# The scaling of the attention probabilities moves to GpSimd in the first 32 of 72 attention steps

## The chip, the cores and the metric

The kernel runs on one core of a Trainium2 chip. Time is device microseconds (us) of one execution; the kernel before took 945.74 us (median of three runs, 944.77 to 946.35). One execution was recorded by the hardware profiler; its rows are used below. PE is TensorE, DVE VectorE, ACT ScalarE, POOL GpSimd; SP issues the DMAs.

## The reference, cut to what matters

```python
# q, k, v: (4, 8, 576, 64) float32
scores = q @ k^T / sqrt(64) - 2**-(h+1) * |i - j|      # head h, masked to 0 <= i - j < 128
attn   = exp(scores - max(scores))
attn   = attn / (sum(attn) + 1e-9)                       # the normalisation in question
x      = (attn @ v) as (2304 tokens, 512)
x      = relu(x @ w1_in)**2 @ w1_out                     # 512 -> 2048 -> 512
h      = x @ w2_in
out    = (h * cos(h)) @ w2_out
```

All in float32.

## The kernel before, in words

**Attention.** The 2304 tokens are 18 tiles of 128; the 8 heads are 4 pairs. One attention *step* (`a`, or `s`) is one tile and one pair of heads, so there are 72 steps, four to a tile. Step a does, in `scores` (L309): matmuls on PE into a bank of PSUM (tile `s_a`), for each of the two heads one custom DVE reduction (L367: adds the bias table, finds the row's extreme), and one ACT exponential (L377) that writes the probabilities `p_a` to SBUF and the row sums to a small tile `st_a`. `normalise` (L386) then makes 1/(sum + 1e-9) on DVE with two instructions on 128x2 (L389, L390), and multiplies each head's 128x256 probabilities by it (L393): two `tensor_scalar` instructions per step, on DVE, over 128 columns in the first tile's four steps, 192 in steps 20 to 23 (tile 5) and 256 elsewhere. `transposes` (L395) turns the four 128x128 blocks on PE (`t_a`) and ACT copies them back into `p_a` (L404). `values` (L407) multiplies by v (`o`); after four steps ACT and DVE split the tile's result into a rounded part `xh` and a rest `xl` (L433, L434), the operands of the first layer.

**MLPs.** A unit i is 128 of the 2048 hidden columns by 512 tokens: 12 matmuls (`h_i`, L463 to L465: three products of rounded parts and rests for each of four slices), the activation, and 12 more (`y`, L524 to L526). The weights arrive as 64-bit floats and are converted piecewise: a POOL memset of a buffer `cv_w` (L168), an ACT cast (L175), a DVE shift-and-or (L179), an ACT cast to the rounded part `wh` (L192) and a DVE subtraction for the rest `wl` (L196). There are two `cv_w` buffers, so a memset waits for the `wl` of two pieces before.

**Order.** The code first runs the *start stage*: steps 0 to 15 back to back, scores up to two steps ahead (`LOOK`). From step 16 on, one step is woven into each unit; steps 16 to 31 lie beside units 0 to 15. The code gives a priority; a scheduler then builds a fixed order of instructions for each engine, with waits on semaphores, from estimated costs, so an edit can move instructions of all engines. Each engine then works through its own list in that order; a waiting instruction holds up all behind it.

**Buffers that tie steps together.** `st` has four buffers: the reductions of step a+4 can't begin until step a's multiplications have read `st_a`. The keys of tile 3 and the keys and queries of tiles 4 and later come by DMA through two buffers `raw_a` (`kq_job`, L251): ACT casts them into `KS` and `qh` (L264, L277, L278), DVE subtracts (`KS`, L265 and L282; `ql`, L283), and only then can the load two further on begin. Below, raw_a0 to raw_a3 are the four loads for tile 3 and raw_a4 to raw_a7 those for steps 16 to 19.

Of the kernel before, what the change touches and what calls it, by code (L numbers as in the profile page):

```python
# [15 lines left out]
ALU = mybir.AluOpType  # L16
# [53 lines left out]
def attention_mlp_mlp(ctx: ExitStack, tc: tile.TileContext, kq, k0, q0, v, w1, w2, bias, ident, out):  # L70
# [7 lines left out]
    te, act, dve, pool, sp = nc.tensor, nc.scalar, nc.vector, nc.gpsimd, nc.sync  # L78
# [216 lines left out]
    def kind(j):  # L295
        return {0: "first", 4: "straddle", 5: "after"}.get(j % 9, "plain")
# [89 lines left out]
    def normalise(a):  # L386
        j, hp = divmod(a, 4)
        pt, st = Pt[a], St.pop(a)
        dve.tensor_scalar(st[:, 4:6], st[:, 2:4], 1e-9, None, ALU.add)  # L389
        dve.reciprocal(st[:, 6:8], st[:, 4:6])  # L390
        c0, c1 = {"first": (0, 128), "after": (64, 256)}.get(kind(j), (0, 256))
        for e in range(2):
            dve.tensor_scalar(pt[:, e, c0:c1], pt[:, e, c0:c1], st[:, 6 + e : 7 + e], None, ALU.mult)  # L393

    def transposes(s):  # L395
        j, hp = divmod(s, 4)
# [184 lines left out]
    with ExitStack():  # L581
# [43 lines left out]
        while s < start_steps:  # L625
            scores_to(min(s + LOOK, start_steps))
            normalise(s)
            transposes(s)
            tick("aw" if s < START_W else "a")
            values(s)  # L630
            s += 1
# [8 lines left out]
        for i in range(len(ORDER)):  # L640
# [9 lines left out]
            if todo > 0:  # L650
                scores_to(s + 1)
                normalise(s)
# [29 lines left out]
            for _ in range(todo - 1):  # L682
                scores_to(s + 1)
                normalise(s)
                transposes(s)
                tick()
                values(s)
                vdone[0] = s + 1
                s += 1
# [57 lines left out]
```

## Time and profile before

| | |
|---|---|
| median of three runs | 945.74 us |
| the profiled execution | 946.06 us, of which the profiler's span is 944.3 us |
| PE busy | 921.9 us, 98% of the span |
| DVE, ACT, POOL busy | 599.4, 522.9, 43.3 us |
| start stage | to about 54 us; there PE is idle for about 14 us |

A share of busy time is an average over the stages; the end of a matmul is modelled, so a busy PE isn't PE at its peak. "Granted clock" is a share of full speed.

### The profile page before, as it was taken

To read this page: it belongs to the slowest core of one execution; us is meant where nothing else is said; L and a number is where in the kernel's file an instruction comes from. 1 tells how busy PE (TensorE), PEld (TensorE's weight loads), DVE (VectorE), ACT (ScalarE), POOL (GpSimd) and SP (SyncE) were. 2 spreads that over 40 slices of the span, in tenths; PEclk is the share of its full clock that TensorE was granted. 3 is DMA by queue.
4 is the path that set the end of the run, shared out by engine and by line. 5 is a ranking of instruction groups with operands and counts; after the bars stand their busy time and mean duration, and the time that the engine had idled before them with its cause. 6 is when DMAs were issued, how large, how long until landed. Compare 5 with 4: busy or idle time off the path is not lost.

```text
span 944.3 us, 13513 instructions
## 1 busy us (share of the span) xinstructions
PE 921.9 (98%) x4992; PEld 768.4 (81%) x4992; DVE 599.4 (63%) x1403; ACT 522.9 (55%) x1134; POOL 43.3 (5%) x100
## 2 busy tenths in 40 slices
PE   7789999999999999999999999999999999999998
PEld 6567777778787888878888888888888888888898
DVE  4988896666657655555655686566556555655564
ACT  4988885554556645455545574454445444444443
POOL 2011110000000000000101100000000000000000
PEclk9999999999999999999999999999999999999999
DMA  7545663320112111123342440011001000100010
GB/s 215 190 168 190 213 219 98 108 68 34 56 57 101 45 38 53 46 85 116 121 147 89 158 155 1 1 45 45 1 1 40 5 1 1 45 1 1 1 45 23
DMA packets 33954, 71.44 MB, mean 76 GB/s; under 512 B 3424, under 2 KB 10976, under 8 KB 33888
## 3 DMA queue, kind: packets, MB, share of 16 engines
q1 hardware_dynamic: 33888, 70.58, 22.6%
q8 instruction: 39, 0.64, 0.3%
q14 instruction: 27, 0.22, 0.1%
HBM read 61.13 MB, written 9.44 MB: 75 GB/s over the span
## 4 chain that ended last, share of the span: by engine, by line
PE 88%; ACT 4%; DVE 4%; DMA 3%; issue 1%; SPq 0%; POOL 0%; ACTq 0%; DVEq 0%
PE h L464 13%; PE h L463 13%; PE h L465 13%; PE y L524 13%; PE y L525 13%; PE y L526 13%; PE s L335 3%; PE o L419 3%; PE t L402 2%; DMA raw_a<-kq_in 2%; ACT p L377 1%; PE s L324 1%; DVE s L367 1%; ACT cv_w L175 1%; DVE cv_w L179 1%
## 5 line engine op out<-in xcount | busy, mean ns | idle before, releaser
L463 PE MATMUL h<-xh,wh 128*128 128x512 f32 (+1 forms) x640 | 237.3, 371 | 0.6 <-ACT xh L433 0.4
L464 PE MATMUL h<-xl,wh 128*128 128x512 f32 (+1 forms) x640 | 236.8, 370 | 0.3 <-DVE xl L434 0.3
L465 PE MATMUL h<-xh,wl 128*128 128x512 f32 (+1 forms) x640 | 236.3, 369 | 0.0
L463 PEld LDWEIGHTS h<-xh,wh 128*128 128x128 f32 x640 | 121.2, 189 | 20.2 <-ACT a L469 0.7
L465 PEld LDWEIGHTS h<-xh,wl 128*128 128x128 f32 x640 | 121.1, 189 | 20.3
L464 PEld LDWEIGHTS h<-xl,wh 128*128 128x128 f32 x640 | 121.1, 189 | 19.0 <-DVE xl L434 0.7
L524 PE MATMUL y<-rh,wh 128*128 128x512 f32 (+1 forms) x320 | 122.5, 383 | 0.8 <-DVE ysb L539 0.8
L525 PE MATMUL y<-rl,wh 128*128 128x512 f32 (+1 forms) x320 | 118.5, 370 | 0.0
L526 PE MATMUL y<-rh,wl 128*128 128x512 f32 (+1 forms) x320 | 118.4, 370 | 0.0
L524 PE MATMUL y<-gh,wh 128*128 128x512 f32 (+1 forms) x320 | 117.8, 368 | 0.0
L525 PE MATMUL y<-gl,wh 128*128 128x512 f32 (+1 forms) x320 | 117.7, 368 | 0.0
L526 PE MATMUL y<-gh,wl 128*128 128x512 f32 (+1 forms) x320 | 117.7, 368 | 0.0
L492 ACT ACTIVATE r<-r 128x512 f32<-128x512 f32 x72 | 45.4, 631 | 120.0 <-DVE r L491 120.0
L377 ACT ACTIVATE p<-s,st 128x256 f32<-128x256 f32 (+4 forms) x160 | 70.6, 443 | 49.3 <-DVE st L367 47.3
L503 DVE TENSOR_TENSOR gl<-r,gh 128x512 fp32r<-128x512 f32 x72 | 49.8, 691 | 75.1 <-ACT gh L502 75.0
L367 DVE CUSTOM_DVE_ANT_0 s<-s,bias_sb 128x256 f32<-128x256 f32 (+4 forms) x160 | 62.1, 392 | 55.5 <-PE s L335 27.1
L489 DVE SCALAR_TENSOR_TENSOR r<-kk,h 128x512 f32<-128x512 int32 x72 | 49.4, 687 | 68.0 <-ACT kk L488 68.0
L488 ACT ACTIVATE kk<-h 128x512 int32<-128x512 f32 x72 | 43.0, 597 | 75.6 <-PE h L465 75.5
L480 DVE TENSOR_TENSOR a<-a 128x512 f32<-128x512 f32 x62 | 42.8, 691 | 49.0 <-ACT rh L479 46.8
L469 ACT ACTIVATE a<-h 128x512 f32<-128x512 f32 x72 | 42.9, 596 | 51.4 <-PE h L465 50.4
L526 PEld LDWEIGHTS y<-rh,wl 128*128 128x128 f32 x320 | 60.3, 188 | 10.5
L524 PEld LDWEIGHTS y<-rh,wh 128*128 128x128 f32 x320 | 60.4, 189 | 9.9 <-DVE ysb L539 1.3
(60 smaller groups left out, 1389.3 us busy)
## 6 DMA issues: line engine op xcount, KB each, us to landing
raw_w<-w_in SPq DMA_DIRECT2D x64, 511.8 KB, 4.6
raw_a<-kq_in SPq DMA_DIRECT2D x56, 256.0 KB, 2.6
v<-v_in SPq DMA_DIRECT2D x18, 256.0 KB, 3.4
y<-ysb SPq DMA_DIRECT2D x18, 256.0 KB, 2.0
raw_a<-y SPq DMA_DIRECT2D x18, 256.0 KB, 2.7
out<-ysb SPq DMA_DIRECT2D x16, 256.0 KB, 2.5
k<-k_in SPq DMA_DIRECT2D x4, 256.0 KB, 5.5
q<-q_in SPq DMA_DIRECT2D x8, 128.0 KB, 5.6
```

The costliest lines, as they stand in the source:

```text
L367: dve.tensor_tensor_reduce(out=sbank[p0:p1, e, c0:c1], in0=sbank[p0:p1, e, c0:c1], in1=bias_sb[p0:p1, h, b0 + c0 : b0 + c1], scale=-0.125, ...
L377: act.activation(pt[p0:p1, e, c0:c1], sbank[p0:p1, e, c0:c1], AF.Exp, bias=st[p0:p1, e : e + 1], scale=-1.0, accum_out=st[p0:p1, 2 + e : 3 ...
L463: te.matmul(o, wh[:, cs], xh, start=(c == 0 and kt == 0), stop=False, skip_group_check=True)
L464: te.matmul(o, wh[:, cs], xl, start=False, stop=False, skip_group_check=True)
L465: te.matmul(o, wl[:, cs], xh, start=False, stop=(kt == KT - 1), skip_group_check=True)
L488: act.activation(kk, hb, AF.Copy, scale=INV2PI)
L489: dve.scalar_tensor_tensor(r, kk, -C1, hb, ALU.mult, ALU.add)
L492: act.activation(r, r, AF.Abs)
L503: dve.tensor_tensor(rl, r, rh.bitcast(F32), ALU.subtract)
L524: te.matmul(o, wh, gh, start=(first and m % per == 0), stop=False, skip_group_check=True)
L525: te.matmul(o, wh, gl, start=False, stop=False, skip_group_check=True)
L526: te.matmul(o, wl, gh, start=False, stop=last, skip_group_check=True)
```

## The change

In `normalise`, the two multiplications of a step go to POOL for steps 0 to 31: 64 instructions. The reciprocal stays on DVE. The remaining 40 steps are as before.

```diff
         c0, c1 = {"first": (0, 128), "after": (64, 256)}.get(kind(j), (0, 256))
+
+        engine = pool if a < 32 else dve
         for e in range(2):
-            dve.tensor_scalar(pt[:, e, c0:c1], pt[:, e, c0:c1], st[:, 6 + e : 7 + e], None, ALU.mult)
+            engine.tensor_scalar(pt[:, e, c0:c1], pt[:, e, c0:c1], st[:, 6 + e : 7 + e], None, ALU.mult)
```

Two lines are added, so every line below L391 has a number two higher in the changed kernel (L393 is L395, L402 is L404). POOL's list of instructions about the end of its first memsets, before:

```order
L363 MEMSET p_18_768 64x2x128
L168 MEMSET cv_w_0_1_0_667 128x512
L168 MEMSET cv_w_0_1_1_700 128x512
L168 MEMSET cv_w_0_2_0_745 128x512
L168 MEMSET cv_w_0_2_1_789 128x512
```

and at the same place now (`p_0` holds the probabilities of steps 0 and 1, `p_2` those of 2 and 3, and so on):

```order
L363 MEMSET p_18_768 64x2x128
L395 ISA
L395 TENSOR_SCALAR p_0_166<-p_0_166,st_0_167 128x128 x2
L395 TENSOR_SCALAR p_0_166<-p_0_166,st_1_175 128x128 x2
L395 TENSOR_SCALAR p_2_183<-p_2_183,st_2_184 128x128 x2
L395 TENSOR_SCALAR p_2_183<-p_2_183,st_3_211 128x128 x2
L395 TENSOR_SCALAR p_4_234<-p_4_234,st_4_235 128x256 x2
L395 TENSOR_SCALAR p_4_234<-p_4_234,st_5_259 128x256 x2
L395 TENSOR_SCALAR p_6_290<-p_6_290,st_6_291 128x256 x2
L395 TENSOR_SCALAR p_6_290<-p_6_290,st_7_318 128x256 x2
L168 MEMSET cv_w_0_1_0_667 128x512
L168 MEMSET cv_w_0_1_1_700 128x512
```

The multiplications stand in POOL's list among the memsets. The row that reads only ISA is new too: in the built program it is a reload of a library of POOL's code, put once ahead of the first multiplication; the list before has no such row.

PE's list at the start of the attention (`s_4` to `s_6` are scores of steps 4 to 6, `t_0` the transposes of step 0), before:

```order
L324 MATMUL s_4_229<-k0_0_129,q0_1_132 128x128 x2
L402 MATMUL t_0_193<-id_sb_126,p_0_166 128x128
L324 MATMUL s_4_229<-k0_0_129,q0_1_132 128x128
L402 MATMUL t_0_193<-id_sb_126,p_0_166 128x128
L324 MATMUL s_4_229<-k0_0_129,q0_1_132 128x128
L419 MATMUL o_0_205<-p_0_166,v_0_147 64x128 x2
L324 MATMUL s_5_254<-k0_0_129,q0_1_132 128x128 x4
```

and now:

```order
L324 MATMUL s_4_229<-k0_0_129,q0_1_132 128x128 x4
L324 MATMUL s_5_254<-k0_0_129,q0_1_132 128x128 x4
L324 MATMUL s_6_285<-k0_0_129,q0_1_132 128x128 x4
L404 MATMUL t_0_193<-id_sb_126,p_0_166 128x128 x2
L404 MATMUL t_1_220<-id_sb_126,p_0_166 128x128 x2
```

The scores of steps 4, 5 and 6 have moved ahead of the first transposes.

PE's list where the start stage ends and the first unit begins (`h_0`), before:

```order
L335 MATMUL s_17_674<-KS_127,ql_4_1_514 128x256 x2
L463 MATMUL h_0_652<-xh_0_100,wh_0_0_272 128x512
L464 MATMUL h_0_652<-xl_0_101,wh_0_0_272 128x512
L465 MATMUL h_0_652<-xh_0_100,wl_0_0_273 128x512
L463 MATMUL h_0_652<-xh_0_100,wh_0_0_272 128x512
```

and now:

```order
L335 MATMUL s_17_674<-KS_127,ql_4_1_514 128x256 x2
L404 MATMUL t_16_732<-id_sb_126,p_16_596 128x128 x4
L465 MATMUL h_0_652<-xh_0_100,wh_0_0_272 128x512
L335 MATMUL s_18_763<-KS_127,qh_4_2_550 128x256 x2
L335 MATMUL s_18_763<-KS_127,ql_4_2_551 128x256 x2
L466 MATMUL h_0_652<-xl_0_101,wh_0_0_272 128x512
```

The transposes of step 16 and the scores of step 18 now stand ahead of the second matmul of unit 0; before they stood behind unit 0 and behind the first `y` matmuls. From unit 3 on, PE's list is the same in both kernels. On DVE the conversions of unit 1's weights have moved from the middle of the start stage to its end, just ahead of the split of tile 3.

## Rows read from the trace of the kernel before

**Rows 1.** The page, busy time and share of the span

```profile
PE 921.9 (98%) x4992; PEld 768.4 (81%) x4992; DVE 599.4 (63%) x1403; ACT 522.9 (55%) x1134; POOL 43.3 (5%) x100
```

**Rows 2.** Windows: stretch, length, busy per engine (x instructions), granted clock, DMA share, GB/s

```profile
0.00:60.00 60.00, 45.64 (x305) 35.99 (x306) 44.18 (x179) 42.60 (x127) 10.30 (x27) 0.94 0.65 200
60.00:160.00 100.00, 96.05 (x531) 77.78 (x532) 81.17 (x216) 83.62 (x196) 14.54 (x31) 1.00 0.56 184
160.00:944.00 784.00, 780.20 (x4158) 654.65 (x4156) 474.01 (x1008) 396.66 (x812) 18.48 (x42) 1.00 0.16 52
20.00:30.00 10.00, 9.88 (x88) 8.25 (x86) 9.50 (x40) 9.80 (x27) 1.06 (x2) 1.00 0.48 162
30.00:40.00 10.00, 7.65 (x70) 5.63 (x70) 9.48 (x40) 9.26 (x30) 0.00 (x0) 1.00 0.65 208
40.00:50.00 10.00, 5.86 (x46) 4.13 (x44) 8.45 (x28) 7.76 (x23) 1.13 (x2) 0.83 0.32 107
```

Busy times stand in the order PE, PE's weight loads, DVE, ACT, POOL.

**Rows 3.** Timeline of PE: start, length, instruction, idle before and its releaser

```profile
43.99 0.66 PE L419 MATMUL o<-p,v 128*64 128x128 f32 x8 [2.40 <-DVE xl L434]
...
53.94 0.49 PE L463 MATMUL h<-xh,wh 128*128 128x512 f32 x1 [0.36 <-ACT xh L433]
...
54.78 0.73 PE L464 MATMUL h<-xl,wh 128*128 128x512 f32 x1 [0.34 <-DVE xl L434]
```

**Rows 4.** DVE's multiplications to 160 us, by shape: busy, mean ns

```profile
L393 DVE TENSOR_SCALAR p<-p,st 128x256 f32<-128x256 f32 x46 | 15.1, 364 | 0.5
...
L393 DVE TENSOR_SCALAR p<-p,st 128x128 f32<-128x128 f32 x8 | 1.9, 283 | 0.0
```

**Rows 5.** POOL's memsets by shape: busy, mean ns, idle before

```profile
L168 POOL MEMSET cv_w<- 128x512 f32 x64 | 33.8, 529 | 310.1 <-DVE wl L196 296.8 <-DVE st L389 7.1 <-DVE st L390 5.4
L363 POOL MEMSET p<- 64x256 f32 x8 | 2.5, 311 | 0.0
```

**Rows 6.** Timeline, first 10 us: the load of ACT's table, POOL's last memset, DVE's first multiplications

```profile
0.73 1.28 ACT L377 ACT_TABLE_LOAD   x1 [0.73 <-PEq L736]
...
7.18 0.31 POOL L363 MEMSET p<- 64x256 f32 x1
...
9.18 0.48 DVE L393 TENSOR_SCALAR p<-p,st 128x128 f32<-128x128 f32 x2
```

**Rows 7.** The page, DMA issues: count, KB each, median us to landing

```profile
q<-q_in SPq DMA_DIRECT2D x8, 128.0 KB, 5.6
```

**Rows 8.** Timeline: the keys' loads and conversions (SP, ACT, DVE) from 30 us

```profile
30.55 0.42 DVE L265 TENSOR_TENSOR KS<-raw_a,KS 64x256 fp32r<-64x256 f32 x1
...
42.04 6.27 SPq L287 DMA_DIRECT2D raw_a<-kq_in  x3
...
45.10 0.40 ACT L277 CAST KS<-raw_a 128x256 fp32r<-128x256 f32 x1
...
46.56 0.42 DVE L367 CUSTOM_DVE_ANT_0 s<-s,bias_sb 64x256 f32<-64x256 f32 x1 [0.94 <-PE s L335]
...
47.08 0.42 DVE L282 TENSOR_TENSOR KS<-raw_a,KS 64x256 fp32r<-64x256 f32 x1
```

**Rows 9.** Timeline of PE: step 16's transposes, step 18's scores

```profile
58.98 0.60 PE L402 MATMUL t<-id_sb,p 128*128 128x128 f32 x4
...
65.41 0.40 PE L335 MATMUL s<-KS,qh 128*128 128x256 f32 x2
```

**Rows 10.** Timeline about 82 us: DVE's reciprocal of a step, PE's transposes of it

```profile
81.90 0.17 DVE L390 RECIPROCAL st<-st 128x2 f32<-128x2 f32 x1
...
84.60 0.60 PE L402 MATMUL t<-id_sb,p 128*128 128x128 f32 x4
```

**Rows 11.** Timeline: the same DVE instruction alone, then beside a POOL memset

```profile
87.00 0.17 DVE L389 TENSOR_SCALAR st<-st 128x2 f32<-128x2 f32 x1 [0.58 <-ACT p L377]
...
94.83 0.53 POOL L168 MEMSET cv_w<- 128x512 f32 x1 [2.77 <-DVE wl L196]
94.88 0.50 DVE L389 TENSOR_SCALAR st<-st 128x2 f32<-128x2 f32 x1
```

## The prediction, on record before the changed kernel ran

> **What bounds the kernel now.** I read the page first, then windows, then the timeline about the start stage. PE is busy for 98% of the span [rows 1], so only PE's idle time can be saved. The windows say where that lies: PE idles 14.4 us of the first 60, 3.9 us of the next 100 and 3.8 us of the last 784 [rows 2]. The first few of the 14.4 are the wait for the first data. Most of the rest falls at 30 to 60 us, where DVE and ACT are busy for 8 to 9.5 of each 10 us [rows 2] and PE waits for DVE in turn: 2.40 us for the split of a tile, then again before the first unit [rows 3]. The granted clock, 0.83 of full speed in 40 to 50 us against 1.00 before, also shows a PE that stands still too often [rows 2]. So the stage to read is the start stage, steps 0 to 15, which ends with the second matmul of unit 0 at 54.78 us [rows 3]. It is the second that counts: from there PE hardly stops.
>
> From 60 us on DVE is busy 81%, but off the path. I expect nothing from the 16 later steps' relief there (16 x 2 x 0.36 = 12 us of DVE): PE's whole idle time is 3.9 us in that stretch, and the order from unit 3 on is unchanged.
>
> **What is removed.** In the start stage, 8 multiplications of 283 ns and 24 of 364 ns [rows 4]: 2.3 + 8.7 = 11 us of DVE's 44.2 busy in 60 [rows 2]. This is a profiled length with the next instruction overlapping it: two over 128 columns together took 0.48 us [rows 6], so the relief of the queue is nearer 9 us. It lies on the path only where PE waits for DVE.
>
> **What is added.** Three things, none of which the trace shows.
>
> 1. *A multiplication on POOL.* The nearest rows are POOL's memsets, which only write: 311 ns for 256 columns, 529 ns for 512 [rows 5]. The lower bound is 0.31 us (reading costs nothing); the upper is twice 529, 1.06 us. I take 0.53 us, as if it touched 512 columns: 256 read, 256 written. A step then costs POOL 1.06 us. The start stage has one step in 2.85 us (54.78 - 9.18 for 16 [rows 3, 6]), so POOL has the room, and the price is latency: a step's transposes begin some 0.5 us later after the reciprocal than with two DVE instructions.
>
> 2. *The reload of POOL's library.* It stands in POOL's list behind the memset that ends at 7.49 us, and all multiplications stand behind it. The first was needed at 9.18 us [rows 6], so the first 1.7 us are free. The only loading of code or tables that the trace shows is ACT's table, 1.28 us [rows 6]; that is the lower bound. If it needs a transfer from memory, the slowest median from issue to landing is the queries', 5.6 us [rows 7]; twice that, 11.2 us, is the upper bound. I take 5.6: code has to come from memory, and this is the stretch in which those loads were measured. The first multiplication then starts at 7.5 + 5.6 = 13.1 us, 3.9 us late.
>
>    The Trainium skill, in GPSIMD Engine Reference, section 2.1, says that the first call to a freshly loaded kernel costs an extra load of about 6 us, measured as 5.95, with no instruction shown for it. No row here shows it; by that figure the sum below would be 0.35 us worse.
>
> 3. *Waits in other queues.* On POOL the memsets of weight buffers now stand between multiplications. Each waits for a DVE `wl` that stands ahead of the reciprocal for which the next multiplication waits, so a step costs at most one memset more (0.53 us). On SP no load moves past a multiplication; but a `raw_a` load waits for DVE's subtractions, and these have moved.
>
> **What the late start costs.** Until 13.1 us DVE, ACT and PE can do the reductions and exponentials of steps 0 to 3 and the scores of steps 4 to 6, which now stand ahead of the first transposes. Then all of them stop, for want of a free `st`. So PE loses less than 3.9 us: about two and a half steps of scores, some 3 us, are taken ahead. Walking the new orders with the lengths of before, step 8's scores end at about the same time as before (some 21 us), with the transposes of step 4 still owed. From there DVE has less to do.
>
> **Where the gain goes.** The second half of the stage hangs on a chain that the change doesn't shorten: the key loads through two buffers. A load for step 18 is issued at 42.04 us, when step 16's subtraction is done, and its cast begins at 45.10 [rows 8]: 3.1 us a link, four links from raw_a0 to raw_a8. The first link starts with the subtraction at 30.55 us [rows 8]. In DVE's new list that subtraction stands behind the split of tile 1 and the first reduction of step 12, and I put it at 31.7 us, 1.1 us later. On the way the lighter DVE gives this back. Before, DVE stood before step 16's reduction until PE had the scores at 46.56, and only then subtracted step 18's keys at 47.08, 1.6 us after their cast was ready [rows 8]. PE had those scores late because the transposes of step 13 waited for DVE. Now I put step 16's reduction at 43.5, and step 18's subtraction right behind its cast, at 46.4: 0.7 us earlier than before. From there to the second matmul of unit 0 it was 54.78 - 47.08 = 7.7 us; DVE's list between them loses 4 multiplications of before (some 1.2 us), but PE must now first do step 16's transposes, which wait for two POOL multiplications and a memset, and step 18's scores, which together take the 1.0 us back. So the second matmul comes at about 53.9, 0.9 us earlier. What stands ahead of it needn't be done later: four transposes, 0.60 us long with the next matmul overlapping (0.45), and scores of about the same length [rows 9], 0.9 us.
>
> Step 16 to 31: between the end of a step's reciprocal and its transposes the tightest place that I found has 84.60 - 82.07 = 2.5 us [rows 10]; two POOL multiplications, a memset and 0.2 us for the signals are 1.8 us. Nothing is lost.
>
> **Sum.** -0.9 - 0.9 = -1.8 us against the profiled execution's 946.06 us (the span of 944.3 and 1.8 around it): 944.3. That execution was 0.3 us above the median of the runs, so against 945.74 the forecast is 943.9 us: a small gain, just at the edge of what can be told from no change here, 0.2% or 1.9 us.
>
> **The rivals.**
>
> *A. The reload is free.* If the code is resident, or comes in ACT's 1.28 us, the first multiplication starts on time and the late start of 3.9 us is gone. PE had filled 1 us of it with work taken ahead, so 2.9 us more come off: 941.0 us. For it: PE's idle time in 30 to 60 us has room for it. Against: the load would have to be shorter than any transfer here.
>
> *B. The reload is long (slower).* Every microsecond beyond 5.6 passes on whole, since DVE, ACT and PE stop behind `st` and the key chain starts later by the same. At 7.4 us the gain is gone; from 9.3 us on the kernel is slower by over 0.2%. At 11.2 us: 943.9 + 5.6 = 949.5. For it: nothing else on POOL can run behind it, and the loads at this time share the DMA with 200 GB/s of other traffic [rows 2]. Against: only that other loads land in half the time.
>
> *C. POOL and DVE hold each other up (slower).* A DVE instruction of 0.17 us took 0.50 when a POOL memset began 0.05 us ahead of it [rows 11]: it waited the memset out. The multiplications will do the same to DVE's remaining small ones, and be held in turn. If each of the last ten of the start stage loses 0.27 us (half of 0.53) on the path, it is 2.7 us, and 946.6. At 1.06 us a multiplication, 5.3 us: 949.2. For it: the row. Against: DVE has 9 us less to do, so waits on it fall into slack except in the tail.
>
> The skill's SBUF — State Buffer, section "Who interferes with whom", makes this an exclusive lock, and adds that a DVE instruction with two SBUF inputs also contends with a POOL instruction that reads SBUF. With the first [rows 11] agree; the second no row of before can show, as POOL only wrote. By it the subtractions (`wl`, `KS`, `ql`) would be held up as well, which is rival C at its upper price.
>
> That the change doesn't do what it says is excluded: the 64 instructions stand in POOL's list.
>
> **How the numbers follow.** The forecast gets 0.42, with a range of its own of 941.5 to 945.5 (0.31 to 1.06 us a multiplication, the reload 4 to 7 us); it lies astride the edge, so 0.20 of it is faster and 0.22 no change. A 0.20, all faster. B 0.22: 0.18 slower, 0.04 no change. C 0.16: 0.10 slower, 0.06 no change. Together 0.40 faster, 0.32 no change, 0.28 slower. The range, 939.5 to 950.5, takes in A with 1.5 us to spare below, B and C to their upper bounds.
>
> **What would show it.** *Reload:* the first POOL multiplication at about 13.1 us; at 9 us it is A, beyond 17 us B. *Length:* POOL multiplications 0.3 to 1.06 us. *Chain:* the first key subtraction near 31.7 us, step 18's near 46.4. *End of the stage:* unit 0's second matmul near 53.9 us, and afterwards the same distance to the end as before, less 0.9 us. *Lock:* 128x2 instructions on DVE of 0.5 us instead of 0.17 in the start stage. The forecast is wrong if the second matmul comes after 55.7 us, or if PE idles more than 5 us between 60 and 160 us.

## The result, and the profile after

The changed kernel takes 956.41 us (median of 4 runs, 952.66 to 957.83) beside 946.05 us for the kernel before on the same chip: a ratio of 1.0099, 95% interval 1.0076 to 1.0121, or about 9.4 us (7.2 to 11.4) slower. The forecast was 943.9 us with a range up to 950.5. The profiled execution took 957.2 us, 11.1 more than that of before, with a span of 955.4 us. Lines behind L391 of the changed kernel stand two further down: the multiplication is L395, the transposes are L404, the first unit's matmuls L465 to L467.

The page's line of busy times, the answer to [rows 1]. DVE has lost 12 us and POOL has gained 59:

```profile
PE 927.8 (97%) x4992; PEld 769.9 (81%) x4992; DVE 587.0 (61%) x1339; ACT 523.7 (55%) x1134; POOL 102.4 (11%) x164
```

The windows, with the columns of [rows 2]:

```profile
0.00:60.00 60.00, 42.08 (x284) 32.29 (x284) 31.87 (x128) 35.72 (x111) 35.81 (x56) 0.86 0.54 161
60.00:160.00 100.00, 94.29 (x501) 74.06 (x500) 75.57 (x187) 85.86 (x197) 41.87 (x61) 0.97 0.61 197
...
20.00:30.00 10.00, 7.42 (x58) 5.33 (x57) 6.11 (x23) 7.55 (x23) 6.33 (x7) 1.00 0.31 100
30.00:40.00 10.00, 8.21 (x73) 6.03 (x72) 5.54 (x23) 6.85 (x21) 6.04 (x9) 1.00 0.29 86
```

From 20 to 30 us PE has fallen from 9.88 to 7.42, and DVE, which was full at 9.50, to 6.11; ACT has fallen too. POOL itself is busy for only 6.3 of the 10 us. Nobody is full any more: the stage waits on its own chain. How late it ends is read on PE's timeline (start, length, idle before, releaser; compare [rows 3]):

```profile
62.18 0.78 PE L465 MATMUL h<-xh,wh 128*128 128x512 f32 x1
...
64.29 0.63 PE L466 MATMUL h<-xl,wh 128*128 128x512 f32 x1
```

The second matmul of unit 0 comes 9.5 us later than before (64.29 against 54.78), which is most of the 11.1. (Between kernels with another order on PE its time is no measure by itself: other work stands ahead of it.) What POOL's multiplication costs stands in the groups by shape (busy us, mean ns), the answer to [rows 4, 5]:

```profile
L395 POOL TENSOR_SCALAR p<-p,st 128x256 f32<-128x256 f32 x48 | 48.3, 1019 | 37.6 <-DVE st L390 19.6 <-DVE st L389 4.5 <-ACT p L406 4.3
...
L395 POOL TENSOR_SCALAR p<-p,st 128x128 f32<-128x128 f32 x8 | 4.7, 603 | 4.8 <-DVE st L390 4.7 <-DVE st L389 0.2
```

The mean also holds slower ones; over the start stage it is 0.974 us. The fastest, four back to back, last 3.62 us, 0.905 each, in the timeline of all engines about 23 us:

```profile
21.30 3.62 POOL L395 TENSOR_SCALAR p<-p,st 128x256 f32<-128x256 f32 x4 [4.30 <-ACT p L406]
...
22.27 0.44 PE L404 MATMUL t<-id_sb,p 128*128 128x128 f32 x2 [0.16 <-POOL p L395]
23.15 0.43 DVE L367 CUSTOM_DVE_ANT_0 s<-s,bias_sb 128x256 f32<-128x256 f32 x1 [1.76 <-POOL p L395]
...
23.17 0.44 PE L404 MATMUL t<-id_sb,p 128*128 128x128 f32 x2 [0.46 <-POOL p L395]
...
29.65 0.43 DVE L367 CUSTOM_DVE_ANT_0 s<-s,bias_sb 128x256 f32<-128x256 f32 x1 [0.84 <-POOL p L395]
```

Two things are to be seen. PE's transposes follow POOL's multiplications one by one, 0.90 us apart, and PE stands still 0.46 us between them. And DVE's *reduction* of a later step, which has nothing to do with that product, stood 1.76 us and then 0.84 us until POOL was done: it writes the row maximum into a tile `st`, there are four of them, and POOL reads the reciprocal out of the oldest until a step's second multiplication ends. DVE's waits up to 70 us (waited for: us in total, times, longest) have three such waits:

```profile
DVE s L367 <- PE s L324: 12.1, 5, 6.3
DVE st L389 <- ACT p L377: 4.1, 5, 2.2
DVE s L367 <- POOL p L395: 3.7, 3, 1.8
```

The wait for PE's scores grew more. Before, it was

```profile
DVE s L367 <- PE s L324: 6.5, 2, 6.1
```

Without the longest in each, which is the wait for the first data, that is 0.4 us before and 5.8 us now. The chain that ended last before 66 us shows which of the two counts (start, length, what):

```profile
21.30 3.63 POOL p L395 x4
24.97 0.44 PE t L404 x2
25.41 0.34 PE s L324 x4
25.76 0.68 issue
26.44 0.43 DVE s L367
27.01 0.11 DVE st L390
27.29 2.34 POOL p L395 x2
29.67 0.44 PE t L404 x2
```

It goes from POOL's product to PE's transposes of step 5, from there to the scores of step 9, which stand behind those transposes in PE's list, to the reduction of these scores, to the reciprocal of step 6, which stands behind that reduction in DVE's list, and back to POOL. Such rounds make up the chain from 21 to 47 us, and POOL's multiplications are 12.4 of its 66 us. No piece of it leads from POOL to a reduction: the three waits for `st` are there, but not on it. The longest wait of a reduction after the first data shows the path once more, between the transposes of step 9 and the scores of step 12:

```profile
37.32 0.44 PE L404 MATMUL t<-id_sb,p 128*128 128x128 f32 x2 [0.46 <-POOL p L395]
...
37.59 0.83 PE L324 MATMUL s<-k,q 128*128 128x128 f32 x6
...
38.13 0.43 DVE L367 CUSTOM_DVE_ANT_0 s<-s,bias_sb 128x256 f32<-128x256 f32 x1 [2.53 <-PE s L324]
```

An estimate says the same. If all starts are worked out again from the lengths in this trace and the waits in the built program, leaving out only the reductions' waits for POOL, the second matmul stays at 64.29 us (in the start-only, half-columns and two-halves kernels below it stays where it was, too). With POOL's multiplications 0.58 as long, near the forecast's 1.06 us a step, it comes at 58.5 us.

Behind that the key chain is late as well, the answer to [rows 8] (DVE's subtractions, first and step 18's):

```profile
38.65 0.76 DVE L265 TENSOR_TENSOR KS<-raw_a,KS 64x256 fp32r<-64x256 f32 x2
...
54.62 0.42 DVE L282 TENSOR_TENSOR KS<-raw_a,KS 64x256 fp32r<-64x256 f32 x1
```

The reload, on the other hand, cost nothing. The instruction that changes POOL's library (line L395's instructions: shortest, median and longest ns, first and last start):

```profile
L395 POOLq MODIFY_POOL_CONFIG  x2: 4/4/4, 7.4 to 7.4; - x2
```

DVE's first reciprocal and POOL's first multiplication in the timeline, the answer to [rows 6]:

```profile
9.12 0.17 DVE L390 RECIPROCAL st<-st 128x2 f32<-128x2 f32 x1
...
9.49 0.61 POOL L395 TENSOR_SCALAR p<-p,st 128x128 f32<-128x128 f32 x1 [2.03 <-DVE st L390]
```

It ran 0.2 us after its operand was ready and 2.1 us after the reload, of which 2.03 were the wait for DVE.

### The profile page after: what moved, and what is told of

Same layout as the page of the kernel before. It is cut to its first block, busy times and chain, and to the rows that moved or that the text cites. A ratio compares the mean times of both kernels' runs of the same rounds, so it can differ in the third digit from the quotient of the medians.

```text
span 955.4 us, 13544 instructions
## 1 busy us (share of the span) xinstructions
PE 927.8 (97%) x4992; PEld 769.9 (81%) x4992; DVE 587.0 (61%) x1339; ACT 523.7 (55%) x1134; POOL 102.4 (11%) x164
## 4 chain that ended last, share of the span: by engine, by line
PE 86%; ACT 4%; DMA 4%; POOL 2%; DVE 2%; issue 1%; SPq 0%; POOLq 0%; ACTq 0%; DVEq 0%
PE h L466 13%; PE h L465 13%; PE h L467 13%; PE y L526 13%; PE y L527 13%; PE y L528 13%; PE s L335 3%; PE o L421 3%; PE t L404 3%; DMA raw_a<-kq_in 2%; POOL p L395 2%; ACT p L377 1%; ACT cv_w L175 1%; ACT p L406 1%; PE s L324 1%
## 5 line engine op out<-in xcount | busy, mean ns | idle before, releaser
L465 PE MATMUL h<-xh,wh 128*128 128x512 f32 (+1 forms) x640 | 237.6, 371 | 0.4 <-ACT a L471 0.3
L467 PE MATMUL h<-xh,wl 128*128 128x512 f32 (+1 forms) x640 | 236.2, 369 | 0.0
L465 PEld LDWEIGHTS h<-xh,wh 128*128 128x128 f32 x640 | 121.1, 189 | 19.9 <-ACT a L471 1.0
L467 PEld LDWEIGHTS h<-xh,wl 128*128 128x128 f32 x640 | 120.9, 189 | 20.2
```

The source lines that it names most:

```text
L465: te.matmul(o, wh[:, cs], xh, start=(c == 0 and kt == 0), stop=False, skip_group_check=True)
L467: te.matmul(o, wl[:, cs], xh, start=False, stop=(kt == KT - 1), skip_group_check=True)
```

## The experiments

Differences in us are a run's ratio to the kernel before, times 946, with the 95% interval.

### The change in parts, and the reload alone

First half of the change alone, second half alone, and only the reload:

```
start only:   engine = pool if a < 16 else dve
woven only:   engine = pool if 16 <= a < 32 else dve
reload only:  (the kernel before) + pool.tensor_scalar(dummy, dummy, 1.0, None, ALU.mult)   # 128x1
```

> POOL multiplies in steps 0 to 15 only; the 16 later steps stay on DVE. If the loss is made in the start stage, where a step's transposes wait for two POOL multiplications in a row, unit 0's second matmul comes near 64 us as with the whole change, and the time is 8 to 10 us above the kernel before. If the two engines hold each other up wherever POOL reads, about half of the loss goes with the 16 steps left out: +4 to +6.

> POOL multiplies in steps 16 to 31 only. If the loss is made in the start stage: 0 to +2.5 us against the kernel before, with the second matmul of unit 0 within 1 us of 54.8 us. If POOL's reading holds DVE up anywhere: +4 to +6 us. By the prediction's own step (slack of 2.5 us against 1.8): 0.

> The kernel before with one POOL multiplication of a 128x1 scratch tile at the beginning, so that the library is changed and nothing else. If the change of the library is free: within 0.5 us of the kernel before. If it holds back the first transfers (in the changed kernel the bias landed 1.1 us later): +1 us. If it takes as long as the prediction put it, nothing waits for it here except the memsets behind it: 0 to +2 us, and those memsets start near 13 us.

Measured: start only 953.44 us, 1.0076 (1.0058 to 1.0095), +7.2 us; woven only 947.74, 1.0022 (1.0008 to 1.0036), +2.1; reload only 946.54, 0.9999 (0.9986 to 1.0013), 0. The two halves add up to the whole: 7.2 + 2.1 = 9.3. So three quarters of the loss are made in the start stage, with PE's list the same as in the changed kernel. Unit 0's second matmul, start only and then woven only:

```profile
62.62 0.63 PE L466 MATMUL h<-xl,wh 128*128 128x512 f32 x1
```

```profile
53.71 0.80 PE L466 MATMUL h<-xl,wh 128*128 128x512 f32 x1
```

In the reload-only kernel the one multiplication stands between two memsets, with no gap (POOL's timeline):

```profile
4.89 0.52 POOL L604 MEMSET q<- 64x512 f32 x1
5.46 0.21 POOL L606 TENSOR_SCALAR dummy<-dummy 128x1 f32<-128x1 f32 x1
5.61 0.98 POOL L168 MEMSET cv_w<- 128x512 f32 x2
```

The library is changed just ahead of it:

```profile
L606 POOLq MODIFY_POOL_CONFIG  x2: 4/4/4, 5.4 to 5.4; - x2
```

### Shorter and longer multiplications

```
half the columns:  if a < 32: c1 = (c0 + c1) // 2
two halves:        for d0, d1 in ((c0, cm), (cm, c1)): engine.tensor_scalar(pt[:, e, d0:d1], ...)
```

> As the changed kernel, but POOL multiplies only the first half of each head's columns in the 32 steps (the rest stays unnormalised): 0.60 us instead of 0.91 for a full head, 1.2 instead of 1.83 us a step. If the length of POOL's multiplications is what counts: 4 to 6 us below the changed kernel (about +4 to +6 against the kernel before). If it is the order in which the steps now stand, or the hand-over between the engines itself, the length not mattering: within 2 us of the changed kernel (+8 to +10). If the prediction's size had been right (1.06 us a step): between -2 and +1 us against the kernel before.

> As the changed kernel, but each POOL multiplication is made in two of half the width: 4 x 0.60 = 2.4 instead of 1.83 us a step. If the length counts: 0.6 us more in each of some 10 to 13 steps on the chain, +16 to +19 us against the kernel before. If order or hand-over counts: +9 to +11.

Measured: half the columns 949.6 us, 1.0036 (1.0019 to 1.0053), +3.4; two halves 965.35 us, 1.0207 (1.0170 to 1.0243), +19.6. Where nothing holds POOL up, a step's multiplications take 1.2, 1.8 and 2.4 us in the half-columns, the changed and the two-halves kernel; by the mean in the start stage (0.700, 0.974 and 0.681 us each) they take 1.4, 1.95 and 2.7. The loss is +3.4, +9.4 and +19.6 us: 6 and then 10 us more (4 to 6 and 6 to 10 had been expected), by either measure 10 to 17 times what a step takes longer, in a stage of 16 steps. (Their lists differ a little from the changed kernel's, PE's in 54 and 38 of 4667 rows.) The length counts, not the hand-over alone. The first also answers a question to the forecast. Drawn on in a straight line to the 1.06 us that it took, the loss would be between 0 and 2 us, an estimate from these runs, and not a gain of 1.8. The size alone wasn't the whole mistake.

### How many buffers st has

```
after, 8 (or 6):   stp = actx.enter_context(tc.tile_pool(name="stp", bufs=8))
before, 8 (or 3):  the same line, normalisation on DVE
own tile:          rc = rcp.tile([P, 2], ...)        # 8 buffers; st stays at 4
                   dve.reciprocal(rc, st[:, 4:6])
                   engine.tensor_scalar(pt[...], pt[...], rc[:, e : e + 1], None, ALU.mult)
```

> As the changed kernel with 8 buffers for st instead of 4, so that the reductions of later steps need not wait until POOL has read an earlier st. If the wait for st passes POOL's length on to DVE and ACT (the prediction's step on the late start): 3 to 6 us below the changed kernel. If the loss is only that a step's transposes come late and the two banks of scores fill: within 2 us of the changed kernel.

> The kernel before with 8 buffers for st and nothing else: the control for the changed kernel with 8. If 4 buffers cost only where a multiplication is long (POOL's 1.83 us a step): within 1.5 us of the kernel before. If the reductions wait for st in the kernel before too, or the freer order alone is worth as much: -4 to -10 us, and the normalisation on POOL would then still cost about 10 us beside it.

> The changed kernel with 6 buffers for st, between the 4 of the changed kernel (+10 us) and the 8 of the run before (0). A step's scores are made two to three steps ahead and the multiplications of up to two more are pending, so 6 should nearly do: 0 to +3 us. If it was the order that 8 buffers happened to give: anything, up to +10.

> The changed kernel with st still in 4 buffers, but the reciprocals written to a small tile of their own (8 buffers), from which POOL's multiplications read. So st is free when DVE has made the reciprocal, and no reduction waits for POOL. If the loss is that POOL holds st until a step's second multiplication: -2 to +2 us against the kernel before. If only the deeper look-ahead that more st buffers allow takes the loss away, POOL's hold being harmless: +6 to +10 us.

> The kernel before with 3 buffers for st instead of 4, normalisation on DVE. If the number of free st buffers sets the pace of the start stage whatever engine normalises (each buffer fewer lets one step fewer be in flight): +5 us or more, with reductions on DVE that wait. If st binds only where a multiplication takes 0.9 us: 0 to +2 us.

Measured, the kernel before being 1:

```
normalisation on      DVE                       POOL in the first 32 steps
st 3                  1.0046 (1.0029-1.0063)    -
st 4                  1                         1.0099 (1.0076-1.0121)
st 4, own tile        -                         1.0029 (1.0014-1.0044)
st 6                  -                         1.0003 (0.9988-1.0018)
st 8                  0.9970 (0.9954-0.9986)    0.9997 (0.9984-1.0011)
```

With 8 buffers the loss was gone against the kernel before (945.72 us), more than expected. With 6 the instructions stand in the same order as with 8, so that run (946.17 us) is a repetition of it. Among DVE's waits up to 66 us in the changed kernel with 8 there is no reduction any more that waits for POOL. One other wait is put down to POOL, that of the conversion of a weight tile at 23.95 us:

```profile
DVE s L367 <- PE s L324: 10.4, 6, 6.5
...
DVE cv_w L179 <- POOL p L395: 2.4, 1, 2.4
```

But that tile's memset was done at 6.15 us. What ended the wait is ACT's cast of the same tile, done at 23.85, behind a copy of transposes that had waited for POOL (ACT's timeline):

```profile
22.59 0.59 ACT L406 COPY p<-t 128x512 f32<-128x512 f32 x1 [1.21 <-PE t L404]
23.07 0.78 ACT L175 CAST cv_w<-raw_w 128x512 f16<-128x512 bf16 x1
```

The control has to be read with it: the kernel before also gains from 8 buffers, 2.8 us, and is then the fastest of all that compute the whole, 943.65 us; with 3 it loses 4.4, which lies between the two expectations. So the number of `st` buffers counts whichever engine normalises. Where DVE does, it can't be by a wait: DVE makes both the multiplications and the reductions, in the order of its own list, and neither trace shows a reduction that waits for `st`. It is the order that the scheduler builds for so many buffers (8 and 3 change 61 and 75 of PE's 4667 rows).

The own tile for the reciprocals keeps the four buffers and takes away POOL's hold on them: 948.73 us, +2.7, between its two expectations. So the four buffers, with POOL as their last reader, are worth 0.70% or 6.6 of the 9.4 us. That isn't the waiting itself, which wasn't on the chain. The own tile, too, changed the order: PE's list differs from the changed kernel's in 108 rows, and only in 30 from the one for 8 buffers. Between the transposes of steps 6 and 7 both of these lists have 16 rows of scores, of steps 9 to 12, which PE can do while POOL multiplies; the changed kernel's has 2. No run kept the changed kernel's order and took away the hold alone, nor gave the own tile to the kernel before. The rival, the deeper look-ahead of more buffers, thus isn't excluded: it is the likelier of the two.

What is left, 2.7, is what the change costs with 8 buffers on both sides as well (0.9997 against 0.9970, 2.6 us). The second matmul, with the own tile (as early as before, though the whole takes 2.7 us longer), and in the kernel before with 8:

```profile
54.61 0.50 PE L467 MATMUL h<-xl,wh 128*128 128x512 f32 x1
```

```profile
51.30 0.68 PE L464 MATMUL h<-xl,wh 128*128 128x512 f32 x1 [0.22 <-DVE xl L434]
```

### POOL beside DVE without a wait, and what the relief is worth

```
dummy beside DVE:   (before, st 8)  dummy = kp.tile([P, 256], F32)
                    dve.tensor_scalar(pt...)
                    if a < 32: pool.tensor_scalar(dummy[:, c0:c1], dummy[:, c0:c1], st[:, 6 + e : 7 + e], None, ALU.mult)
relief alone:       (before, st 8)  if a >= 32: dve.tensor_scalar(pt...)
relief and dummy:   (before, st 8)  pool.tensor_scalar(dummy...) if a < 32, else dve.tensor_scalar(pt...)
```

> DVE normalises as before; POOL does the same 64 multiplications on a scratch tile that nobody reads (st has 8 buffers so that nothing waits for them). It computes nothing that the output needs. If the price is latency: within 0 to +1.5 us of the kernel before. If it is that POOL and DVE hold each other up: +5 to +10 us, since here DVE is not even relieved of its share.

> The kernel before with 8 buffers for st, and without any normalisation in the first 32 steps (left out; the output lacks it). It is what the relief of DVE alone is worth, POOL having nothing to do. The prediction counted on about 1 to 3 us: 940.5 to 942.5 beside 943.65 for the same with normalisation. If PE doesn't wait for DVE in the start stage once st is free: within 1 us of 943.65.

> The run beside it with POOL making the 64 multiplications on a scratch tile that nobody reads: DVE relieved, POOL as busy as in the changed kernel, but no transposes that wait for it. If what is left of the loss with 8 st buffers (2 to 3 us) is latency: within 1 us of the run beside it. If it is that POOL holds DVE up: 2 to 4.5 us above the run beside it (4.5 was the difference between the same pair with DVE's multiplications in).

Measured: dummy beside DVE 947.91 us, 1.0018 (1.0007 to 1.0029); relief alone 941.25 us, 0.9943 (0.9924 to 0.9963); relief and dummy 941.10 us, 0.9948 (0.9930 to 0.9967).

Unit 0's second matmul with relief alone, then with relief and dummy:

```profile
49.54 0.66 PE L465 MATMUL h<-xl,wh 128*128 128x512 f32 x1
```

```profile
49.96 0.57 PE L467 MATMUL h<-xl,wh 128*128 128x512 f32 x1
```

The dummy beside DVE was run and its expectations were set against the kernel before, where +1.7 us looked like latency and nothing else. Its true control is the kernel before with 8 buffers, whose order on PE, DVE and ACT it shares, and against that it costs 0.48%, 4.5 us: holding each other up is no small thing where DVE still does its own multiplications. DVE's groups to 60 us (busy us, mean ns), first without POOL's work,

```profile
L393 DVE TENSOR_SCALAR p<-p,st 128x256 f32<-128x256 f32 x26 | 8.3, 354 | 0.1
...
L196 DVE TENSOR_TENSOR wl<-cv_w,wh 128x512 fp32r<-128x512 f32 x6 | 4.1, 686 | 0.2
L434 DVE TENSOR_TENSOR xl<-o,xh 128x512 fp32r<-128x512 f32 x4 | 2.8, 690 | 0.0
```

and then with it:

```profile
L393 DVE TENSOR_SCALAR p<-p,st 128x256 f32<-128x256 f32 x26 | 9.9, 415 | 0.1
L196 DVE TENSOR_TENSOR wl<-cv_w,wh 128x512 fp32r<-128x512 f32 x6 | 4.5, 751 | 0.0
L436 DVE TENSOR_TENSOR xl<-o,xh 128x512 fp32r<-128x512 f32 x4 | 2.8, 690 | 0.0
```

The multiplications (354 to 415 ns) and `wl`, with two inputs in SBUF (686 to 751: two of the six took 0.88 us), are held up; `xl`, whose first input lies in PSUM, is not (690 and 690, two of the four beside POOL's multiplications). That is as the Trainium skill has it in SBUF — State Buffer, section "Who interferes with whom", and shows the part of it, two SBUF inputs against POOL's reads, that the trace of before couldn't. These rows are 2 us of DVE's time to 60 us; what makes up the rest of the 4.5 isn't shown (memsets of weight buffers stand behind POOL's dummy work, too).

The last pair, again of one order on PE, DVE and ACT, answers it for the change itself: with DVE relieved POOL's work beside it costs 0.9948 - 0.9943 = 0.05%, 0.5 us, which isn't told from nothing. The relief alone is worth 0.9970 - 0.9943 = 0.27%, 2.6 us, the other order that it brings included (PE's list differs in 145 rows). So with 8 buffers the change costs 0.9997 - 0.9948 = 0.49%, 4.6 us, and what differs between the two is that the transposes wait for POOL's product (their orders differ too, PE's in 117 rows).

### Sharing the work

```
columns:  pool.tensor_scalar(pt[:, e, c0:c0+64], ...); dve.tensor_scalar(pt[:, e, c0+64:c1], ...)
heads:    (dve if e else engine).tensor_scalar(...)                           # st 8
start:    engine = pool if a < 16 else dve                                    # st 8
```

> In the 32 steps POOL multiplies 64 columns of each head (by the fitted length 0.29 + 64 x 0.0024 = 0.45 us, 0.9 a step) and DVE the other 192 (64 in steps 0 to 3) beside it. If POOL's length counts: close to the kernel before, -1 to +2 us. If the two engines hold each other up when both work on the same tile: +4 us or more.

> In the 32 steps POOL multiplies head 0 and DVE head 1, side by side, 8 buffers for st: a step's latency is 0.91 us (POOL) beside 0.36 (DVE), instead of 1.83. If a step's latency is all that matters once st is free: -2 to 0 us against the kernel before. If the two engines hold each other up when they work on the same tile: +2 to +4 us (sharing by columns with 4 buffers was +5).

> POOL multiplies in steps 0 to 15 only, with 8 buffers for st. If the wait for st is the whole loss of the start stage: -1 to +1 us against the kernel before. If the 16 later steps cost something apart from st: below the changed kernel with 8 buffers by that, about 1 us.

Measured: columns 950.78 us, 1.0050 (1.0031 to 1.0069); heads 945.23 us, 0.9991 (0.9979 to 1.0003), as expected of the shorter latency; start only, 8 buffers, 945.58 us, 0.9992 (0.9979 to 1.0005). With the columns every multiplication became one on each engine; POOL's of 64 columns took 585 ns on average, not the 450 expected, and the loss of 4.7 us, with 4 buffers, speaks for the second expectation without showing which part of it is which. Sharing by heads with 8 buffers is 2.0 us behind DVE alone with 8. The half of the change that lies in the woven steps can't be told from nothing with 8 buffers (0.9997 against 0.9992). No division between the engines beat DVE alone with as many buffers.

## Why the prediction was wrong

**What bounds the kernel** was right: the loss lies where PE's idle time lies, and the end of the start stage carries it. The second matmul as the sign of it was right, and both limits set for a wrong forecast were passed: it came at 64.29 us, later than 55.7, and PE idled 100 - 94.29 = 5.7 us between 60 and 160. The second 0.9 us of the sum, for work done ahead of the second matmul, didn't show either: 9.5 us late there became 11.1 at the end.

**What is removed** was of the right size: the sum had a gain of 1.8 us left from it, and the relief alone, with nothing added, gave 2.6 (taken with 8 buffers, and in another order).

**The multiplication on POOL** is the step that failed. It was put at 0.53 us, from memsets of 512 columns, and is 0.905, inside its bounds of 0.31 to 1.06 and near the upper one. A step's pair takes 1.8 instead of 1.06 us. The half-columns kernel, with 1.2, gave 6.0 of the 9.4 us back. The rest lies in the sentence "POOL has the room, and the price is latency". Room was there (6.3 of 10 us busy); but the price was not 0.5 us once. The latency is paid on a loop, round after round: POOL's product, the transposes, the scores behind them in PE's list, their reduction, the next reciprocal behind it in DVE's list, and POOL again, with 12.4 us of multiplications on the chain to 66 us. The prediction looked for the price where a step is late, and not at what stands behind that step in PE's list. It did see a stop of all engines, "for want of a free `st`", yet only for a late reload. The `st` counts all the time, though by the order that the scheduler builds for four of them and not, as far as the chain shows, by a wait: the own tile, which leaves the size and gives another order, gave 6.6 of 9.4 back. The 6.0 and the 6.6 are two ways to open the same loop and don't add up.

**The reload** was put at 5.6 us and cost 0 (reload only: 0.9999, its multiplication at 5.46 us behind a change of library at 5.40). Rival A's mechanism was what happened, without its time. By the Trainium skill, GPSIMD Engine Reference, section 2.1, it would have been some 6 us; neither run shows that, and the measurement decides.

**The key chain** was expected 1.1 us late at its first link and 0.7 early at step 18's; it was 8.1 late (38.65 against 30.55) and 7.5 late (54.62 against 47.08). It didn't set the delay, it passed it on: DVE came to the first subtraction late because the reduction ahead of it had waited 2.53 us for PE's scores, at 38.13 us.

**Steps 16 to 31**, "nothing is lost", was wrong by 2.1 us with 4 buffers (woven only). Its arithmetic had 1.8 us in a slack of 2.5 at the tightest place found, and left out `st` there as well; with 8 buffers nothing is lost that could be told (0.9997 and 0.9992). Whether it is `st` in these steps, and by which way, stays open: the orders differ, and between 60 and 170 us of the woven-only kernel neither DVE nor PE waits for POOL.

**Rival C** had the sign and not the mechanism. The signs that it named are there, `wl` and the multiplications held up in the dummy kernel, yet with DVE relieved they cost 0.5 us, which isn't told from nothing.

The account, each term from a pair of runs: relief -2.6, holding each other up +0.5, transposes that wait +4.6, the four `st` with POOL as reader (by the order, mostly or wholly) +6.6. Together +9.1 against +9.4 measured. The first three were taken with 8 buffers, the fourth with 4; that they add up says only that what is left with the own tile, 2.7, is as much as the change costs with 8 buffers, 2.6. Each is uncertain by 2 us or so, and all but the second include a change of order.

Open is how much of the loss the clock makes. At the end of the start stage of the changed kernel PE, after being busy for 2.56 of the 4 us from 50 to 54, ran at the lower level (0.50, 1.2 GHz) for 12 us:

```profile
50.00:54.00 4.00, 2.56 (x22) 1.93 (x22) 3.82 (x12) 3.76 (x13) 2.26 (x2) 0.89 0.63 194
54.00:58.00 4.00, 3.06 (x20) 1.96 (x17) 3.47 (x11) 3.69 (x10) 2.15 (x2) 0.50 0.57 193
58.00:62.00 4.00, 3.22 (x17) 2.13 (x16) 2.86 (x7) 2.90 (x7) 2.57 (x4) 0.50 0.63 200
62.00:66.00 4.00, 3.70 (x12) 2.80 (x13) 2.61 (x8) 3.15 (x8) 0.26 (x1) 0.50 0.22 71
```

In the kernel before, the one such stretch there:

```profile
54.00:58.00 4.00, 3.65 (x9) 2.67 (x10) 3.85 (x12) 3.07 (x8) 0.53 (x1) 0.61 0.56 207
```

PE's busy 9.98 us of the 12 would be 5 at the full clock; before, 0.39 x 3.65 = 1.4 us were lost so. By this estimate up to 3.6 us of the profiled 11.1 are the clock's. It came behind PE's waits, and lies within the terms above; no run held it fixed. (The lower level was also granted from 12.19 to 19.02 us, but there 16 matmuls of scores took 3.78 us, 0.24 each, as 12 did before at 1.00 in 2.93 us.) The executions say a little: the four of the changed kernel had a mean granted clock of 0.986, 0.987, 0.989 and 0.994 and took 957.83, 957.20, 955.63 and 952.66 us; the eight of the kernel before with 0.994 have a median of 946.2. So at one clock some 6.4 us are left, by a single execution.

## What to carry to other kernels

Before work moves to another engine, list what stands behind its consumer in every list: here PE's scores behind the transposes, so that a slower product came back to its own engine in each round. List every buffer that the moved instruction reads, too, as well as the one that it writes: a scheduler builds its order around a small tile of scalars with few copies as much as around the data. A wait that a trace shows isn't yet the cause: the reductions waited 3.7 us for `st`, and the chain that ended last didn't pass there. Off-loading an engine that isn't the bound saves only what stands on the path (here 2.6 us, for some 23 us of DVE's work in 32 steps), while the new engine's whole latency enters a chain that has no slack. And a control must have the same buffers and order as the run that it judges: the dummy run looked harmless until it was held against the kernel before with 8.

## What the runs showed that was not expected

The fastest version is the kernel before with one number changed: 8 buffers for `st`, 943.65 us, 0.9970 (0.9954 to 0.9986), with nothing moved. On POOL a multiplication by a scalar for each partition takes 0.60 us for 128 and 0.905 us for 256 columns, 0.3 us and 2.4 ns a column, where DVE takes 0.28 and 0.36 us. Changing POOL's library cost nothing that could be seen: 0.2 us from operand to start in the changed kernel, and 0.06 us from the change to the multiplication in the one with the reload alone.
